# Attention with a Sinkhorn block sort, then a mixture of experts: one modality load, q ahead of v, and row scatters spread over attention units

## Chip, cores, metric

The kernel runs on one core of a Trainium2 chip. The metric is the device time of one execution in microseconds (us). Several executions are timed, and medians are given. An execution more than 1.5% above the fastest of the same kernel is called slow; the others are fast, and only fast ones enter a ratio. The ratio of two kernels is the mean time of one kernel's fast runs over the mean of the other's in the same rounds on the same chip, so it is not quite the ratio of the medians that are quoted beside it.

This case needs one more caution, which the experiments found: the chips, or something else that changes from one call of the experiments to the next, differ. In some calls the kernel before takes 244 to 247 us (medians), in others, on three other chips, 231 to 233. Every run below is therefore set against runs of the kernel before on its own chip, and the kind of chip is named.

## What is computed

The reference, cut to what matters:

```python
for _ in range(5):                                   # Sinkhorn, 32 (batch, head) pairs, 8x8 blocks
    P = softmax(P, axis=-1);  P = P / (P.sum(axis=-2) + 1e-9)
k_sorted = einsum('bhij,bhjcd->bhicd', P, k_blocks)  # same for v
attn = softmax(q_block @ k_sorted_block.T / 8)       # 96x96 blocks, head_dim 64
x = (attn @ v_sorted_block)  ->  3072 rows of 512
logits = x @ w_gate + modality_bias[modality_id]     # 8 experts
e_idx = argmax(logits);  gate = softmax(logits)[e_idx]
out[row] = gate * (relu(x[row] @ w1[e]) @ w2[e])     # 512 -> 1024 -> 512
```

## The kernel before

The work comes in two groups of 16 attention units (a unit is one head, half of its blocks, two batches). Group 0's k and v are sorted on PE, then units 0 to 15 run, with group 1's sort in between. Eight units make a chunk of 768 finished rows. For each chunk the kernel *chooses* the expert of each row on DVE, *ranks* the rows with matmuls (tile `rk`), writes them with eight indirect DMAs to an expert-ordered scratch in HBM, and computes from the expert counts a *table* of slots: blocks of 256 rows of one expert. A slot's rows come back by two transposing DMAs into `xT`. Hidden matmuls (`hp`) and output matmuls (`yp`) of the slots, "pieces", are put between the attention units from unit 17 on. Slots 0 and 1 come from chunk 0, 2 and 3 from chunk 1, 4 to 7 from chunk 2, 8 to 12 from chunk 3.

Loads at the start, all small ones on SP's queue, the large ones on POOL's:

```python
nc.sync.dma_start(out=P_t, ...)            # sort net
nc.sync.dma_start(out=BT[:, 0:2], ...)     # gate bias per modality, to all partitions, 8 KB
nc.sync.dma_start(out=wg_sb, ...)          # gate weights
for t in range(6):                         # modality ids, 4 bytes apiece
    nc.sync.dma_start(out=modI[...], in_=<every 12th id>)
...
load_k(0, 0); load_k(0, 1); load_v(0); load_q(0, 0); load_q(0, 1)
```

The first operations on `BT` are wedged between the Sinkhorn's own operations on DVE:

```python
gap = [ ..., [..., lambda: V.tensor_reduce(mA[:, 0:1], BT[:, 0], AX.X, ALU.max)], ...]
for it in range(5):
    nc.scalar.activation(P_t, P_t, ACT.Exp)
    for f in gap[it]:
        f()
    nc.vector.tensor_reduce(red, P_t, AX.X, ALU.add)   # ... the Sinkhorn goes on
```

The scatters of a chunk, one after the other on POOL, and the schedule:

```python
for t in range(8):
    if t:
        nc.gpsimd.nop()
    ins = nc.gpsimd.indirect_dma_start(out=xs_dram, out_offset=<dest[:, t]>, in_=<rows t>)
# ... cut
at2(8 * m + 9, place, m) if m == 0 else at1(8 * m + 10, place, m)
at1(8 * m + 10, table_x, m) if m == 0 else at2(8 * m + 10, table_x, m)
# after the loop:  at1(10, late_loads)

def late_loads():                          # second half of group 1's q, second expert's weights
    first = load_q(1, 1)
    tc.add_manual_dep(first.ins, xins[0].ins.name, SYNC, reason="rows of the first slot go ahead")
    load_w(1)
```

`at1(u, ...)` is the place in unit u ahead of its attention-value product, `at2` the one behind.

The softmax here doesn't subtract the row's maximum and nothing guards it: scores larger than these inputs give would overflow.

## Time and profile before

| | before |
|---|---|
| median of 3 runs | 245.98 us (245.48 to 247.62) |
| profiled span, mean granted clock | 243.9 us, 0.82 |
| PE busy | 70% |
| DMA packets under 512 B | 21,951 of 33,247 |

Two rows of the page, the engines' busy time and the chain of work that ended last, complete what the prediction shows:

```profile
PE 170.2 (70%) x2011; PEld 124.3 (51%) x2022; DVE 103.6 (42%) x344; ACT 91.9 (38%) x145; POOL 72.5 (30%) x100
...
PE 49%; issue 9%; another core or an unknown queue 8%; DVE 4%; ACT 3%; DMA 1%; POOL 0%; POOLq 0%; DVEq 0%; ACTq 0%
```

PE is busy 70% of the span, yet the chain has only half of its time on PE. "An unknown queue" at 8% means that an engine was released by an event which no recorded work explains: these are the late completion counts of PE that the prediction describes. (An engine raises a count, a semaphore, when an instruction is done, and the engines that need the result wait for this count. A count is called late where the trace records it well after the end of its instruction.)

### The profile page before, as it was taken

How to read it: one execution, taken by the hardware profiler on the slowest of the kernel's cores; microseconds unless marked ns; L12 is line 12 of the kernel's file. 1: busy time of each engine (PE TensorE's matmuls, PEld its weight loads, DVE VectorE, ACT ScalarE, POOL GpSimd, SP SyncE). 2: the span in 40 equal slices, each digit the busy share in tenths (PEclk: the TensorE clock that was granted, in tenths of full speed). 3: DMA queues.
4: the chain of work that ended last, by engine and by line, in shares of the span. 5: the costliest groups of instructions: out<-in, count | busy, mean ns of one | idle time of the engine just before them, and what ended most of it. 6: DMA issues, size and time to landing. Idle time of an engine off the chain costs nothing.

```text
span 243.9 us, 5078 instructions
## 1 busy us (share of the span) xinstructions
PE 170.2 (70%) x2011; PEld 124.3 (51%) x2022; DVE 103.6 (42%) x344; ACT 91.9 (38%) x145; POOL 72.5 (30%) x100
## 2 busy tenths in 40 slices
PE   0059619478544997929999854999990899999700
PEld 0059517377433886715766631667750467665300
DVE  6858626157720778502664703344630122232300
ACT  2028516536423685524624522354410323222200
POOL 7301070300074400473030571303275133223310
PEclk9999655558755579785999997699998699999975
DMA  5999999994022699524320223632053663222200
GB/s 81 214 222 176 213 226 196 217 209 77 0 69 66 102 187 208 103 81 108 84 89 3 102 81 78 157 60 89 17 171 119 135 155 84 86 86 78 82 26 0
DMA packets 33247, 27.64 MB, mean 113 GB/s; under 512 B 21951, under 2 KB 28863, under 8 KB 32960
## 3 DMA queue, kind: packets, MB, share of 16 engines
q0 software_dynamic: 11760, 23.10, 42.6%
q1 hardware_dynamic: 21456, 4.14, 10.8%
q8 instruction: 18, 0.29, 0.5%
q14 instruction: 13, 0.11, 0.1%
HBM read 27.33 MB, written 10.52 MB: 155 GB/s over the span
## 4 chain that ended last, share of the span: by engine, by line
PE 49%; issue 9%; another core or an unknown queue 8%; DVE 4%; ACT 3%; DMA 1%; POOL 0%; POOLq 0%; DVEq 0%; ACTq 0%
PE hp L624 18%; PE yp L647 17%; PE va L321 2%; PE gt L402 2%; PE lg L408 2%; PE op L389 2%; PE sc L370 2%; PE tq L354 1%; DMA xs_scratch<-xb,dest 1%; DVE xb L393 1%; ACT qT L618 1%; PE ypl L677 1%; PE hl L663 1%; ACT xTg L299 1%
## 5 line engine op out<-in xcount | busy, mean ns | idle before, releaser
L624 PE MATMUL hp<-xT,w 128*128 128x256 bf16 x384 | 50.2, 281 | 7.6 <-ACT qT L618 7.6
L638 POOL DMA_INDIRECT out_dram<-kvb,idg x25 | 24.4, 976 | 72.1 <-ACT kvb L634 30.4
L624 PEld LDWEIGHTS <-w 128*128 128x128 bf16 x384 | 37.0, 101 | 15.5 <-issue 7.8
L476 POOL DMA_INDIRECT xs_scratch<-xb,dest x32 | 29.3, 917 | 48.1 <-issue 48.1
L376 ACT ACTIVATE attnT<-sc 96x768 bf16<-96x768 f32 x32 | 25.7, 804 | 9.1 <-PE sc L370 3.5
L647 PE MATMUL yp<-w,qT 128*128 128x512 bf16 x91 | 25.1, 407 | 4.8 <-ACT qT L618 2.6
L647 PE MATMUL yp<-w,hT 128*128 128x512 bf16 x90 | 24.7, 414 | 0.3
L393 DVE TENSOR_TENSOR xb<-op,rs 96x512 bf16<-96x512 f32 x32 | 22.0, 687 | 1.1
L392 DVE RECIPROCAL rs<-op 96x8 f32<-96x8 f32 x32 | 6.4, 199 | 37.2 <-PE op L389 10.8
L618 ACT ACTIVATE qT<-hp 128x512 bf16<-128x512 f32 x16 | 9.4, 597 | 25.2 <-remote 13.3
L408 PE MATMUL lg<-wgp,xTg 128*96 128x8 bf16 x128 | 9.5, 198 | 13.2 <-ACT xTg L299 10.8
L634 ACT ACTIVATE kvb<-yp,idg 128x512 f32<-128x512 f32 x13 | 8.9, 686 | 24.0 <-PE yp L647 18.4
L636 DVE TENSOR_SCALAR kvb<-yp,idg 128x512 f32<-128x512 f32 x11 | 8.3, 751 | 22.8 <-PE yp L647 22.8
L299 ACT COPY qT<-tq 128x768 bf16<-128x768 bf16 x14 | 11.2, 797 | 17.0 <-PE tq L354 16.6
L647 PEld LDWEIGHTS <-qT 128*128 128x128 bf16 x96 | 9.3, 102 | 15.0 <-issue 4.4
L618 ACT ACTIVATE hT<-hp 128x512 bf16<-128x512 f32 x18 | 10.6, 594 | 15.5 <-PE hp L624 15.3
L389 PE MATMUL op<-v_sb,attnT 96*128 96x65 bf16 x256 | 16.0, 214 | 0.4 <-DVE xb L393 0.4
L408 PEld LDWEIGHTS <-xTg 128*96 128x96 bf16 x128 | 8.6, 146 | 14.5 <-ACT xTg L299 11.4
L354 PE MATMUL tq<-ident,q_il 128*128 128x128 bf16 x96 | 11.0, 271 | 6.9 <-DVE q_il L128 6.8
L389 PEld LDWEIGHTS <-attnT 96*128 96x128 bf16 x256 | 13.7, 111 | 3.4 <-DVE xb L393 0.7
L647 PEld LDWEIGHTS <-hT 128*128 128x128 bf16 x96 | 9.7, 105 | 10.4 <-issue 2.9
L370 PE MATMUL sc<-qT,kT 64*128 64x96 bf16 (+1 forms) x256 | 13.6, 237 | 1.6 <-DVE qT L299 0.7
(172 smaller groups left out, 219.7 us busy)
## 6 DMA issues: line engine op xcount, KB each, us to landing
w<-in_moe_w_dram POOLq DMA_DIRECT2D x4, 1024.0 KB
kvb<-in_k_dram POOLq DMA_DIRECT2D x4, 768.0 KB
kvb<-in_v_dram POOLq DMA_DIRECT2D x2, 1536.0 KB
v_sb<-in_q_dram POOLq DMA_DIRECT2D x4, 384.0 KB
q_in<-in_q_dram POOLq DMA_DIRECT2D x4, 384.0 KB
xs_scratch<-zpad SPq DMA_DIRECT2D x3, 258.0 KB
xs_scratch<-xb,dest POOLq DMA_INDIRECT x32
out_dram<-kvb,idg POOLq DMA_INDIRECT x25
```

Of the source, the lines that this page charges most:

```text
L299: (nc.scalar.copy if pick(act, dve) else nc.vector.tensor_copy)(dst, src)
L354: nc.tensor.transpose(tp[:, t], src[:, t], ident)
L370: nc.tensor.matmul(sc[0:m, par, j * BLK:(j + 1) * BLK], kT[g][rows, x0:x0 + m], qT[rows, i], start=True, stop=True)
L376: nc.scalar.activation(attnT[u % 2][:, 0:8 * BLK].rearrange("p (r f) -> p r f", r=2), sc_tiles.pop(u)[0:BLK, :, 0:4 * BLK], ACT.Exp, scale ...
L389: nc.tensor.matmul(ov[:, par, j], attnT[u % 2][:, c0:c0 + 128], v_sb[g][0:BLK, par * 64 + h * 8 + i, 0:D + 1], start=True, stop=True)
L393: nc.vector.tensor_tensor(xt[:, :, h * D:(h + 1) * D].rearrange("p (r j) d -> p r j d", r=2), ov[0:BLK, :, :, 0:D], rs.broadcast_to([BLK, ...
L408: nc.tensor.matmul(lg[:, t], xTg[c % 2][:, t], wgp[:, c], start=True, stop=True)
L476: ins = nc.gpsimd.indirect_dma_start(out=xs_dram, out_offset=bass.IndirectOffsetOnAxis(ap=dest[:, t:t + 1], axis=0), in_=xt.bitcast(I32)[: ...
L618: nc.scalar.activation(dst, src, ACT.Relu)
L624: nc.tensor.matmul(hp[:, f], w_at(s, c * F + (2 * j + f) * 128, 128), xT_b[s % NX][:, c], start=(c == 0), stop=(c == 3))
L638: ins = nc.gpsimd.indirect_dma_start(out=out, out_offset=bass.IndirectOffsetOnAxis(ap=idg[:, t, 0:1], axis=0), in_=y, in_offset=None, boun ...
L647: nc.tensor.matmul(yp, hT_b[s % 2][:, fc, t * 128:(t + 1) * 128], w_at(s, 4 * F + fc * Dm, Dm), start=(fc == 0), stop=(fc == 7))
```

## The change

The intent: the 4-byte modality pieces, which slow all other loads of the head, become one contiguous load and a transposition on PE; q comes ahead of v, so that attention starts before the v sort; and the eight scatters of a chunk, which stall PE's consumers when issued in a burst, leave one by one. The core of the diff:

```diff
     nc.sync.dma_start(out=P_t, ...)
+    modI = xTg[1].rearrange("p a b -> p (a b)").bitcast(I32)[0:NTL, 0:2 * BLK]
+    nc.sync.dma_start(out=modI, in_=<32 rows of 768 bytes>)
     nc.sync.dma_start(out=BT[:, 0:2], ...)
     nc.sync.dma_start(out=wg_sb, ...)
-    for t in range(6): nc.sync.dma_start(out=modI[...], ...)
...
+    load_q(0, 0)
     load_v(0)
-    load_q(0, 0)
     load_q(0, 1)
...
+            after = [mark[0].ins] if t else []          # mark: the last exponential or ReLU
+            for pre in after:
+                tc.add_manual_dep(ins.ins, pre.name, SYNC, reason="rows leave at an even pace")
...
-            at2(8 * m + 9, place, m) if m == 0 else at1(8 * m + 10, place, m)
-            at1(8 * m + 10, table_x, m) if m == 0 else at2(8 * m + 10, table_x, m)
-    at1(10, late_loads)
+            if m == 0:
+                at2(9, place, 0)
+                for t in range(1, 8):
+                    at1(9 + t, lambda t: ones_[0](t), t)
+                at1(16, table_x, 0)
+                at1(16, late_loads)
+            else:
+                at1(8 * m + 10, place, m)
+                for t in range(1, 8):
+                    (at2 if t % 2 else at1)(8 * m + 10 + t // 2, lambda t, m: ones_[m](t), t, m)
+                at1(8 * m + 14, table_x, m)
...
-    run_pieces(2)
+    for t in range(1, 8):
+        run_pieces(1)
+        ones_[3](t)
     table_x(3)
```

Cut: the transposition of the modality ids, the gate weights' product moved behind the k sort with its reduction on DVE, units 0 and 1 moved into the v sort, and a guard that holds a piece back while its slot has no table.

More of the change, by code (lines that the diff above doesn't have):

```diff
@@ L98 @@
     nc.sync.dma_start(out=P_t, in_=sort_net.rearrange("b h i j -> (b h) i j"))
+    mod_w = moe_modality_id.tensor.reshape(list(moe_modality_id.tensor.shape)).bitcast(I32).ap()
+    modI = xTg[1].rearrange("p a b -> p (a b)").bitcast(I32)[0:NTL, 0:2 * BLK]
+    nc.sync.dma_start(out=modI, in_=bass.AP(tensor=mod_w.tensor, offset=mod_w.offset,
+                                            ap=[[2 * BLK, NTL], [1, 2 * BLK]]))
     nc.sync.dma_start(out=BT[:, 0:2], in_=moe_modality_bias.rearrange("(o m) e -> o m e", o=1).broadcast_to([128, 2, E]))
@@ L101 @@
     nc.sync.dma_start(out=wg_sb, in_=moe_w_gate.rearrange("(c p) e -> p c e", p=128))
-    mod_w = moe_modality_id.tensor.reshape(list(moe_modality_id.tensor.shape)).bitcast(I32).ap()
-    modI = singles.tile([BLK, NTL], I32)
-    for t in range(6):
-        src = bass.AP(tensor=mod_w.tensor, offset=mod_w.offset + 2 * t,
-                      ap=[[12, 16], [2 * BLK, NTL], [1, 1]])
-        nc.sync.dma_start(out=modI[t * 16:(t + 1) * 16].rearrange("p (a o) -> p a o", o=1), in_=src)
     k_src = k.rearrange("b h (n c) d -> (b h n) (c d)", n=NB)
@@ L195, in perm_mult @@
         eng.tensor_tensor(tmp, a, p_, ALU.mult)
-        nc.vector.tensor_reduce(dst, tmp, AX.X, ALU.add)
+        return lambda: nc.vector.tensor_reduce(dst, tmp, AX.X, ALU.add)
     V = nc.vector
@@ L261, in home_map, with mod_rows @@
         nc.vector.tensor_tensor(perm, hb, sF8.broadcast_to([128, E, E]), ALU.is_equal)
-        perm_mult(BTp, BT, "b")
+        perm_mult(BTp, BT, "b")()
         nc.vector.tensor_copy(etab, BTp[0:1, 3])
     biasm = singles.tile([BLK, NTL, E], FP32)
+    modB = singles.tile([NTL, 6, 16], BF16)
     modF = singles.tile([BLK, NTL], FP32)
     modN = singles.tile([BLK, NTL], FP32)
+    def mod_rows():
+        src = modI.rearrange("b (r t w) -> b t r w", r=16, t=6)[:, :, :, 0]
+        nc.vector.tensor_copy(modB, src)
+        tp = mipsum.tile([128, 64], BF16, tag="mi", name="modT")
+        nc.tensor.transpose(tp[0:BLK, 0:NTL], modB.rearrange("b t r -> b (t r)"), ident[0:NTL, 0:NTL])
+        nc.vector.tensor_copy(modF, tp[0:BLK, 0:NTL])
+    wgf = small.tile([128, 4, E], FP32, tag="wgf", name="wgf")
     def gate_consts():
-        wgf = small.tile([128, 4, E], FP32, tag="wgf", name="wgf")
-        perm_mult(wgf, wg_sb, "w")
-        nc.gpsimd.tensor_copy(wgp, wgf)
-        nc.gpsimd.tensor_copy(modF, modI)
+        red_w = perm_mult(wgf, wg_sb, "w")
         nc.gpsimd.tensor_scalar(modN, modF, -1.0, 1.0, ALU.mult, ALU.add)
@@ L282, in gate_consts, with rest_w @@
         nc.gpsimd.tensor_tensor(biasm, biasm, tmp, ALU.add)
+        def rest_w():
+            red_w()
+            nc.vector.tensor_copy(wgp, wgf)
+        return rest_w
     busy = [0.0, 0.0]
@@ L375, in expo @@
     def expo(u):
-        nc.scalar.activation(attnT[u % 2][:, 0:8 * BLK].rearrange("p (r f) -> p r f", r=2),
+        mark[0] = nc.scalar.activation(attnT[u % 2][:, 0:8 * BLK].rearrange("p (r f) -> p r f", r=2),
                              sc_tiles.pop(u)[0:BLK, :, 0:4 * BLK], ACT.Exp, scale=scale)
@@ L439 @@
     scat = {}
+    ones_ = {}
+    mark = [None]
     def place(m):
@@ L472, in place, with one @@
         use(dve=1.5)
-        for t in range(8):
+        def one(t):
             if t:
@@ L478, in place @@
                 in_=xt.bitcast(I32)[:, t], in_offset=None)
-            tc.declare_no_dep(ins.ins, group="xs", reason="rows are disjoint")
+            after = [mark[0].ins] if t else []
+            tc.declare_no_dep(ins.ins, group="xs", reason="rows are disjoint", **({"keep": after} if after else {}))
             tc.add_to_no_dep_group("xs", ins.ins)
+            for pre in after:
+                tc.add_manual_dep(ins.ins, pre.name, SYNC, reason="rows leave at an even pace")
             scat[m].append(ins.ins)
+        ones_[m] = one
+        one(0)
         nxt = ohs[(m + 1) % 2]
@@ L615, in relu @@
         if not pick(0.61, 0.7):
-            nc.vector.tensor_scalar(dst, src, 0.0, None, ALU.max)
+            mark[0] = nc.vector.tensor_scalar(dst, src, 0.0, None, ALU.max)
         else:
-            nc.scalar.activation(dst, src, ACT.Relu)
+            mark[0] = nc.scalar.activation(dst, src, ACT.Relu)
     def mL1(s, j):
@@ L701 @@
     use(dve=0.5)
+    mod_rows()
     make_upper_triangular(nc, maskUT, val=1.0, diag=False)
@@ L704 @@
     g0 = jobs(0, [s_, o_, m_, m_, m_, m_, s_, o_,
-                  m_, m_, s_, m_, m_, o_, m_, m_, m_, m_, o_, m_, m_])
+                  m_, m_, o_, m_, m_, o_, m_, m_, o_, m_, m_, o_])
+    hold = []
     for n, (f, g, x0, kd) in enumerate(g0):
@@ L710 @@
             use(dve=2.0)
+            load_k(1, 0)
+            load_k(1, 1)
+            hold.append(gate_consts())
+            prep_s(0)
+            prep_q(0)
+            prep_q(1)
+            scores(0)
+            expo(0)
             make_bd(1)
             late_consts()
-            load_k(1, 0)
-            load_k(1, 1)
-        if n == 13:
-            prep_s(0)
-        if n == 16:
-            prep_q(0)
-            scores(0)
-            expo(0)
+        if n == 12:
+            scores(1)
+            expo(1)
+    hold[0]()
     load_v(1)
@@ L723 @@
     load_w(0)
-    gate_consts()
-    prep_q(1)
     zero_block()
@@ L797, in run_pieces @@
             f, a = pieces[st["pos"]]
+            if (f is mL1 and a[0] >= st["x"]) or (f is last_L1 and SL >= st["x"]):
+                return
             f(*a)
@@ L811 @@
         p1, p2 = pace(u)
-        if u:
+        if u > 1:
             scores(u)
```

## The prediction

> **What bounds the kernel now.** I read the page first, then the chain of waits, then stretches of the timeline. The page says that TensorE (PE) is the busiest engine, but in bands:
>
> ```profile
> PE   0059619478544997929999854999990899999700
> PEclk9999655558755579785999997699998699999975
> DMA  5999999994022699524320223632053663222200
> ```
>
> PE's row has holes (slices 6, 8, 12, 24, 31), and the clock row drops to half around each. I asked for engine busy time in six stretches that the timeline shows without matmuls:
>
> ```profile
> core 0: us, PE busy (x) PEld busy (x) DVE busy (x) ACT busy (x) POOL busy (x), PEclk, DMA share, GB/s
> 30.80:36.00 5.20, 0.03 (x1) 0.00 (x0) 1.01 (x4) 0.80 (x1) 4.34 (x7) 0.50 1.12 225
> 45.30:50.10 4.80, 0.00 (x0) 0.00 (x0) 1.02 (x3) 1.10 (x2) 2.46 (x6) 0.50 1.19 224
> 70.30:76.70 6.40, 0.05 (x1) 0.05 (x2) 0.00 (x0) 1.89 (x3) 4.84 (x6) 0.50 0.29 82
> 105.40:109.80 4.40, 0.00 (x0) 0.00 (x0) 0.00 (x0) 1.60 (x2) 3.49 (x4) 0.85 0.31 90
> 143.20:150.30 7.10, 2.17 (x14) 0.79 (x14) 1.11 (x3) 1.24 (x3) 3.39 (x4) 0.94 0.25 70
> 182.50:190.20 7.70, 0.06 (x2) 0.03 (x1) 0.47 (x1) 0.68 (x2) 3.54 (x4) 0.79 0.44 133
> ```
>
> Length less PE busy: 5.2 + 4.8 + 6.3 + 4.4 + 4.9 + 7.6 = 33.2 us of idle PE. The waits name them:
>
> ```profile
> DVE wgf L196 <- POOL ptmpw L195: 4.2, 1, 4.2
> POOL modF L273 <- DMA modI<-in_moe_modality_id_dram: 10.5, 1, 10.5
> ACT qT L618 <- remote: 13.3, 2, 8.1
> DVE qT L616 <- remote: 10.3, 1, 10.3
> ```
>
> Hole one: the gate weights' product stands in POOL's queue behind loads that wait for the v sort. Hole two: the modality ids (2 KB pieces, 20.5 us to landing) end at 46.4. The other four are the four bursts of eight row scatters, one burst per chunk of attention. In burst one:
>
> ```profile
> 70.91 0.91 POOL L476 DMA_INDIRECT xs_scratch<-xb,dest  x1 [0.30 <-issue]
> 75.75 0.91 POOL L476 DMA_INDIRECT xs_scratch<-xb,dest  x1 [0.30 <-issue]
> 76.65 0.80 PE L408 MATMUL lg<-wgp,xTg 128*96 128x8 bf16 x8 [6.35 <-ACT xTg L299]
> 78.59 1.34 SPq L591 DMA_TRANSPOSE xT<-xs_scratch  x1
> 78.67 0.20 DVE L392 RECIPROCAL rs<-op 96x8 f32<-96x8 f32 x1 [9.69 <-PE va L321]
> ```
>
> DVE waits 9.7 us for a matmul group that ended at 70.30. In the trace's semaphore records, PE's completion counts normally appear at once; during a burst they appear at 69.98, 72.89, 75.78 and 78.64, one per 2.9 us, while ACT's and DVE's own counts are prompt. So consumers of PE starve, then PE. Output scatters 1.9 us apart (123.91, 125.82) delay nothing.
>
> **What the Trainium skill says.** "DMA: Bandwidth & Descriptors", Rules for kernel authors: a non-contiguous last dimension becomes one descriptor per element. The trace agrees: about 3,200 packets of 4 bytes, nearly all between 18 and 48 us. Same page, Queues, rings and completion order: an engine alternates between queues at packet granularity. The trace agrees: these small packets drain only as fast as the large loads beside them. "SBUF — State Buffer", SBUF: two separate sides: only DVE and GpSimd share a port, as a lock. That does not explain the bursts: ACT also stalls, and DVE ran its table arithmetic during 177.0 to 179.3, beside scatters. "TensorE: Matmul & The Clock Gate", Part 1: the clock halves after an idle window of about 3.4 us and recovers after a busy one. The drops agree; recovery here takes 3.6 us (190.2) to 11.3 us (76.7).
>
> **The change, part by part**, on that trace's clock.
>
> *Head.* Modality becomes one load of 32 rows, transposed on PE (about 0.4 us before the k sort); hole two, 4.8 us, goes. The gate product moves early; hole one goes as a wait. But q's first half now precedes v in one queue. Before, v landed at 19.97, q's first half at 24.83; the same bytes in the new order put v at about 25. The v sort started at 20.4; I now start it at 25.6, after the first scores (home map 2.0 us, spread 0.6, transposes, copies). Its remaining 55 matmuls at half clock take 0.12 us each (20 took 2.37), so it ends, with the second scores, at 33.6 instead of 30.2. Then evacuation, reduce, spread: unit 2's scores at 37.6 instead of 38.43. Gain **0.8**, not 5. With the modality, **5.6**.
>
> *Chunk 0.* One scatter per unit: burst one's 6.3 goes, and sooner recovery of the clock gives perhaps 1.5. Units 11 to 16 then end **13.5** earlier.
>
> *The price of spreading.* The last of those scatters waits for unit 16's exponential, which ends at T (92.6 before, 79 after). Before, the last scatter (75.75) to the first slot's transposed rows (81.76) took 6.0 us. The first slot's matmuls come 0.85 us after T in PE's order, so PE waits about 5.2 us. The second half of group 1's q waits for those rows too: it is issued 0.6 us later, and landed 8.4 us after issue (82.36 to 90.78), so at T+15.1. DVE's spread of it stands ahead of chunk 1's choice: 0.6 + 1.5 us more, the rank matmuls at T+17.3. They were at T+5.4 (97.98): **−11.9**. From there to the second slot's first matmul took 16.4 us with burst two in it; without it, at half clock at first, about 12.8: **+3.6**. Net so far **+5.2**.
>
> *Chunk 1.* Scatters every half unit to unit 21, table in unit 22, rows needed in unit 23. Table arithmetic 1.75 us, address load 1.3, transposed rows 3.2: about 2 us late. **−2**.
>
> *Chunk 2.* Its table moves from unit 26 to unit 30, but its slot 4 was due in unit 29, so the new guard skips unit 29's pieces. The last scatter waits on unit 29's exponential and queues behind two output scatters; PE then waits 7 us for slot 4. Burst three's 4.9 us hole and its half clock go, a 7 us hole and its half clock come: **about 0**.
>
> *Chunk 3.* Scatters alternate with pieces of 0.9 or 1.7 us, and two output scatters lie between: ten on POOL at 1.2 us, nearly a burst again, though each waits for a relu and so throttles itself. Rank matmuls to slot 8 took 22.0 us; I get 15 to the last scatter plus 6.1, so 21, followed by half clock as before: **0 to −1**.
>
> Strict sum: 5.2 − 2 − 0.5, about 2.7, so 243. I chose 241: several debits are taken in full, while a PE without holes in the first 60 us could regain full clock earlier (it ran at 0.5 from 26.5 to 57.2), each window of 3.4 us of it worth 1.7.
>
> **Rivals.** (1) The holes simply go: 33 us less, and some clock: 210 to 215. For it: the scatters' pace is slower than any that stalled. Against: the program order above. It needs row loads and q to be early, and they are moved late. (2) Late rows and late q cost more than the bursts did: 250 or more. For it: 11.9 + 2 + 7 + 6 nearly equals the 23 us of bursts. Against: the modality wait and burst one go for certain, and little takes their place. (3) Even spread scatters delay PE's counts: a few us worse everywhere; the output scatters speak against it. (4) Loads bound the head: then removing 3,000 small packets matters. The page has DMA at 9 tenths to slice 8, but the k sort and v sort of group 1 run well after their data land (36.2, 43.6), so only v of group 0 is affected.
>
> **Range and chances.** The clock (±3), the slot 0 chain (±3), chunks 2 and 3 (±4 together) give about ±6, somewhat wider downward, as rival 1 is partly right if q lands sooner. 2% faster is 241.06, just beside my number: faster 0.47, same 0.46, slower 0.07.
>
> **What would show it.** Right: no wait on the modality load; the v sort starting near 25; no "remote" waits of 5 us or more in the attention; PE waiting 4 to 6 us at the first hidden matmuls, then DVE waiting 6 to 8 us for q's load at unit 17; a hole of about 6 us before slot 4 and one before slot 8. Wrong: rows of slot 0 in time, q landing within 4 us of issue, a v sort not later than before, or full clock through the early units, each worth 3 to 8 us below my number; or PE's counts still late with spaced scatters, above it.

## The result

Median 255.91 us (254.38 to 256.43, 4 runs) against 246.59 us (245.48 to 247.62, 4 runs) for before on the same chip; ratio 1.0368, 95% interval 1.0297 to 1.0439. The change makes the kernel 3.7% slower. The profiled spans are 254.7 and 243.9 us.

The page of the changed kernel, same rows as before:

```profile
PE 170.7 (67%) x2012; PEld 123.6 (49%) x2023; DVE 102.7 (40%) x344; ACT 93.0 (37%) x147; POOL 72.7 (29%) x98
...
PE   0007687957799182998599961399975499999600
PEclk9999589975559656799869997599999579999975
DMA  6999968999111299931511222442134843222200
...
PE 54%; DMA 14%; DVE 13%; ACT 5%; issue 4%; another core or an unknown queue 3%; SPq 1%; POOL 1%; POOLq 0%; DVEq 0%; ACTq 0%
```

PE does the same work. The early holes (before: slices 6, 8 and 12) are gone, but there are new ones at slices 14, 16, 25 to 26 and 31 to 32. In the chain "unknown queue" fell from 8 to 3%, but DMA rose from 1 to 14% and DVE from 4 to 13%. The summary of waits names them (columns: total us, times, longest):

```profile
PE hp L641 <- DMA xT<-xs_scratch: 20.1, 4, 9.9
PE rep L238 <- DVE P_bf L232: 18.3, 1, 18.3
...
PE rk L459 <- DVE oh L443: 7.6, 3, 5.6
...
DVE q_il L125 <- DMA q_in<-in_q_dram: 5.7, 1, 5.7
ACT attnT L385 <- remote: 5.7, 1, 5.7
...
DVE mA L204 <- DMA BT<-n_moe_modality_bias_dram: 4.0, 1, 4.0
```

The first line says that the hidden matmuls wait four times for rows, 20.1 us in all; in before this view has no such line. The last is a wait in the Sinkhorn. The timeline (start, duration, engine, line, work, and in brackets the idle time ahead of it and what ended it) shows the two most costly places:

```profile
89.18 1.87 PE L641 MATMUL hp<-xT,w 128*128 128x256 bf16 x8 [3.97 <-DMA xT<-xs_scratch]
...
89.73 1.62 POOL L118 DMA_DIRECT2D q_in<-in_q_dram  x2 [5.85 <-DMA xT<-xs_scratch]
...
98.29 0.63 DVE L125 COPY q_il<-q_in 128x768 bf16<-128x768 bf16 x2 [5.68 <-DMA q_in<-in_q_dram]
...
100.37 0.23 PE L459 MATMUL rk<-oh,maskUT 96*128 96x64 bf16 x1 [5.60 <-DVE oh L443]
...
157.85 0.81 ACT L385 ACTIVATE attnT<-sc 96x768 bf16<-96x768 f32 x1 [5.67 <-remote]
...
163.35 1.87 PE L641 MATMUL hp<-xT,w 128*128 128x256 bf16 x8 [9.89 <-DMA xT<-xs_scratch]
```

The first slot's rows reach PE 4.0 us late; behind them q's second half is issued at 89.73 and usable at 98.29, and the rank matmuls of chunk 1, in DVE's order behind the copy of q, start at 100.37. The last line is slot 4, rows 9.9 us late. Ahead of it in the program the scatters of chunk 2 and of the output stand in one row on POOL (150.3, 151.6, 152.8, 154.1, 155.4), and PE's counts are late again: in the semaphore records the counts of a score matmul that ended at 153.36 and of the table's matmul at 153.47 were seen 4.4 and 4.3 us after them. So the wait "remote" of 5.67 is the old illness, in a scatter sequence that was meant to cure it.

Where the span went, in sections, from the traces (T is the end of unit 16's exponential; "slot s" the first ReLU of slot s). Positive is a loss. The last column is the same pair of kernels on a chip without late counts:

| section | predicted | measured | on a chip without late counts |
|---|---|---|---|
| start to T | −13.5 | 92.6 → 82.7: −9.9 | 84.8 → 80.9: −3.9 |
| T to slot 1 | +8.3 | 23.3 → 28.9: +5.6 | 19.0 → 28.5: +9.5 |
| slot 1 to slot 2 | +2 | 10.6 → 16.7: +6.1 | 10.6 → 11.9: +1.4 |
| slot 2 to slot 4 | 0 | 30.8 → 37.0: +6.2 | 28.8 → 31.3: +2.6 |
| slot 4 to slot 8 | 0 to +1 | 38.4 → 38.2: −0.1 | 36.1 → 36.4: +0.3 |
| slot 8 to the end | 0 | 48.3 → 51.2: +2.9 | 51.2 → 49.2: −2.0 |

The last section has the same work in both kernels. Asked for engine busy time from slot 8's first matmul to the end, the traces answer, before and after (columns as in the prediction):

```profile
194.50:243.90 49.40, 35.29 (x229) 22.26 (x231) 11.07 (x16) 10.28 (x17) 11.66 (x12) 0.91 0.24 74
```

```profile
201.50:254.70 53.20, 37.87 (x228) 23.41 (x232) 10.24 (x15) 10.37 (x17) 10.68 (x11) 0.85 0.25 70
```

The same matmuls keep PE busy 2.6 us longer at a granted clock of 0.85 instead of 0.91. On the other chip this section went the other way, so it is put down to the phase in which the clock drops fell, not to a part of the change. No run tests that.

### The profile page after: what moved, and what is told of

It reads as the page before. It is cut to its first block, busy times and chain, and to the rows that moved or that the text cites. A ratio compares the mean times of both kernels' runs of the same rounds, so it can differ in the third digit from the quotient of the medians.

```text
span 254.7 us, 5091 instructions
## 1 busy us (share of the span) xinstructions
PE 170.7 (67%) x2012; PEld 123.6 (49%) x2023; DVE 102.7 (40%) x344; ACT 93.0 (37%) x147; POOL 72.7 (29%) x98
## 4 chain that ended last, share of the span: by engine, by line
PE 54%; DMA 14%; DVE 13%; ACT 5%; issue 4%; another core or an unknown queue 3%; SPq 1%; POOL 1%; POOLq 0%; DVEq 0%; ACTq 0%
PE hp L641 17%; PE yp L664 14%; DMA xT<-xs_scratch 5%; PE va L330 4%; DMA BT<-n_moe_modality_bias_dram 3%; PE gt L411 3%; DMA q_in<-in_q_dram 3%; PE lg L417 3%; PE ka L321 3%; PE op L398 3%; PE sc L379 2%; DMA xs_scratch<-xb,dest 2%; DVE xb L402 2%; PE tq L363 2%
## 5 line engine op out<-in xcount | busy, mean ns | idle before, releaser
L641 PE MATMUL hp<-xT,w 128*128 128x256 bf16 x384 | 56.0, 301 | 23.0 <-DMA xT<-xs_scratch 20.1
L641 PEld LDWEIGHTS <-w 128*128 128x128 bf16 x384 | 39.6, 107 | 34.5 <-issue 17.6
L635 ACT ACTIVATE hT<-hp 128x512 bf16<-128x512 f32 x19 | 11.3, 597 | 40.1 <-PE hp L641 39.7
L664 PE MATMUL yp<-w,qT 128*128 128x512 bf16 x91 | 23.6, 391 | 1.6 <-ACT qT L635 1.2
L664 PE MATMUL yp<-w,hT 128*128 128x512 bf16 x90 | 22.7, 386 | 2.5 <-ACT qT L635 2.1
L635 ACT ACTIVATE qT<-hp 128x512 bf16<-128x512 f32 x17 | 10.0, 597 | 20.5 <-PE hp L641 10.6
L651 ACT ACTIVATE kvb<-yp,idg 128x512 f32<-128x512 f32 x14 | 9.6, 685 | 18.7 <-PE yp L664 16.5
L653 DVE TENSOR_SCALAR kvb<-yp,idg 128x512 f32<-128x512 f32 x10 | 7.5, 750 | 21.1 <-PE yp L664 21.1
L330 PE MATMUL va<-bd,kvb 128*128 128x128 bf16 x128 | 14.5, 284 | 1.0 <-DVE v_sb L308 0.6
L398 PEld LDWEIGHTS <-attnT 96*128 96x128 bf16 x256 | 13.5, 110 | 3.4 <-DVE xb L402 0.8
L308 ACT CAST v_sb<-va 96x512 bf16<-96x512 f32 (+1 forms) x19 | 11.8, 657 | 7.8 <-PE va L330 6.9
L330 PEld LDWEIGHTS <-kvb 128*128 128x128 bf16 x128 | 13.1, 189 | 1.4 <-issue 1.1
L379 PE MATMUL sc<-qT,kT 64*128 64x96 bf16 (+1 forms) x256 | 12.8, 227 | 0.7 <-ACT qT L308 0.2
```

Of the source, the lines that this page charges most:

```text
L308: (nc.scalar.copy if pick(act, dve) else nc.vector.tensor_copy)(dst, src)
L330: nc.tensor.matmul(acc[:, z], v_cols[:, d0 + z], bd[g], start=True, stop=True)
L379: nc.tensor.matmul(sc[0:m, par, j * BLK:(j + 1) * BLK], kT[g][rows, x0:x0 + m], qT[rows, i], start=True, stop=True)
L398: nc.tensor.matmul(ov[:, par, j], attnT[u % 2][:, c0:c0 + 128], v_sb[g][0:BLK, par * 64 + h * 8 + i, 0:D + 1], start=True, stop=True)
L635: mark[0] = nc.scalar.activation(dst, src, ACT.Relu)
L641: nc.tensor.matmul(hp[:, f], w_at(s, c * F + (2 * j + f) * 128, 128), xT_b[s % NX][:, c], start=(c == 0), stop=(c == 3))
```

## The experiments

Theory A: three delays that the change itself makes (the gate-bias table behind the modality load; q's second half behind the first slot's rows; late tables in the later chunks) outweigh what the head and the bursts give. Rival B: spread scatters as such hold the engines. Rival C: the new order of the large loads is the cost. All results are correct. Chips: the first call ran on a chip with late counts, all later calls on three chips without; the changed kernel was first measured on a chip with late counts, perhaps the same one.

| run | edit, in words | median, us | before on that chip | ratio (95%) |
|---|---|---|---|---|
| e1_bt_first | changed kernel, gate-bias table first | 248.35 | 244.01 | 1.0147 (1.0058–1.0236) |
| e2_head_only | head of the change alone | 241.75 | 244.01 | 0.9934 (0.9864–1.0004) |
| e3_spread_only | spreading alone | 255.61 | 244.01 | 1.0439 (1.0352–1.0527) |
| e4_q_early | changed kernel, q's second half early | 244.11 | 244.01 | 0.9976 (0.9888–1.0064) |
| e5_bt_q | both repairs | 228.47 | 231.37 | 0.9932 (0.9825–1.0039) |
| e6_spread_c0 | both, only chunk 0 spread | 227.14 | 231.37 | 0.9859 (0.9765–0.9954) |
| e7_bursts | both, all in bursts | 225.42 | 231.37 | 0.9779 (0.9665–0.9893) |
| e8_two | as e7, at most two in flight | 240.81 | 231.37 | 1.043 (1.027–1.059) |
| e9_after | changed kernel | 240.06 | 232.22 | 1.033 (1.0246–1.0414) |
| e10_bt_q | as e5 | 229.06 | 232.22 | 0.9858 (0.9777–0.9939) |
| e11_bursts | as e7 | 225.0 | 232.22 | 0.9714 (0.9629–0.9799) |
| e12_before | before, for its trace | 232.16 (one run) | 232.22 | – |
| e13_c23_burst | changed kernel, chunks 2 and 3 in bursts | 238.57 | 231.66 | 1.0185 (1.0087–1.0283) |
| e14_modality | before, contiguous modality load fourth | 234.11 | 231.66 | 1.0076 (1.0004–1.0147) |
| e15_bursts | as e7 | 224.91 | 231.66 | 0.9697 (0.9614–0.978) |
| e16_flights | as e7, another number in flight per chunk | 244.05 (one run) | 231.66 | – |
| e17_modality_third | before, contiguous modality load third | 226.97 | 232.47 | 0.9765 (0.968–0.9849) |
| e18_defer | as e7, no pieces in units 29 and 30 | 219.35 | 232.47 | 0.9368 (0.9266–0.947) |

The profiled executions of e1, e4, e13 and e18 were slow.

**e1_bt_first**

```diff
-    nc.sync.dma_start(out=modI, ...)
     nc.sync.dma_start(out=BT[:, 0:2], ...)
+    nc.sync.dma_start(out=modI, ...)
```

> The changed kernel with the gate-bias table's load put back ahead of the modality load. Theory A (the loss is a sum of three delays that the change itself makes: the gate-bias table late in the Sinkhorn, the rows of the first slot and the second half of q late after unit 16, and the tables of the later chunks late): the table lands near 4.5 us, the block matrix is ready near 15.3 instead of 19.3, and the total falls by 3 to 4 us, to about 252. It falls less if the modality load, now later, is waited for instead (it is read just before the k sort). Rival B (spread scatters as such hold the engines) and rival C (q ahead of v is the cost): no change, 255 to 256.

From 1.0368 to 1.0147 of before: 2.2%, or 5.4 us of 244. The wait on the table is gone, and the Sinkhorn's last product releases PE 4.1 us earlier than the 18.3 shown above:

```profile
PE rep L238 <- DVE P_bf L232: 14.2, 1, 14.2
```

T comes at 79.0 instead of 82.7, and the modality load, now third, lands 4.1 us after issue and is waited for by nobody. The fast profile of the same head (e10) has the same 14.2. The two ratios come from two calls, perhaps two chips; e9 and e10 below repeat the shift on one. Theory A holds here; B and C, which expected nothing, fall for this part.

**e2_head_only and e3_spread_only**

```diff
 e2: the scatter loop, the places of place, table_x and late_loads as in the kernel before
 e3: the kernel before with the new scatter loop, its places, late_loads at unit 16, the guard
```

> The changed kernel's head, with the scatters, tables and late loads as they were before. Theory A: the gain of 5.7 us at unit 6 stays, with the four bursts as before, so about 241 (240 to 242). Rival C (the new order of the loads in the head is the cost): 250 or more. Rival B: also about 241, as the spread scatters are gone.

> The kernel before with the spread scatters and their tables alone, head untouched. Theory A and rival B: the spreading costs what the change lost less what its head gained, about 15 us: 258 to 262. Rival C: 246 or faster, as the head is the old one.

The head alone is 0.7% faster (the interval just includes no gain), the spreading alone, with q's second half held back as in the change, 4.4% slower, and 0.9934 × 1.0439 = 1.037, the change itself. So the loss is in the second half of the change; rival C falls as the main cause. The head brought the start of unit 6's exponential from 54.6 to 48.9, against the trace of before from the first measurement. How much of that is left at the end is open: within the call the means differ by about 1.6 us (0.7% of 244), while the one execution profiled, the fastest of four, has a span 5.5 us below that older trace. The four bursts are there in both kernels. The summary of waits of e2 has, for one of them, 10.1 us with no recorded releaser:

```profile
DVE qT L628 <- remote: 10.1, 1, 10.1
```

**e4_q_early**

```diff
     load_q(1, 0)
     load_w(0)
+    load_q(1, 1)
+    load_w(1)
...
-                at1(16, late_loads)
```

> The changed kernel with the second half of group 1's q and the second expert's weights loaded right behind the first expert's, not behind the rows of the first slot. Theory A: DVE's wait of 5.7 us for q at unit 17 goes; the rank matmuls of chunk 1 come near T+10 instead of T+17.7 (T is the end of unit 16's exponential), what is left being the wait for the first slot's rows; total 248 to 251, less if the added 2.7 MB hold up the loads of group 1's k and v. Rival B: nothing to gain from q, 254 to 256.

From 1.0368 to 0.9976: 3.9%, or 9.6 us, the largest single piece. (The edit loads the second expert's weights early too; the wait that goes is the one for q.) The wait for q is gone, and in its profile the rank matmuls come at T+11.6. PE's counts were still over 4 us late in chunk 2. The fast pair e9 and e10 below shows the same.

**e5_bt_q, e6_spread_c0, e7_bursts, e8_two**

```diff
 e5: e1 and e4 together
 e6: + for t in range(8 if m in (1, 2, 3) else 1): one(t)      # and the tables of before
 e7: + the same with chunk 0
 e8: e7, and  + after = [scat[m][t - 2]] if t >= 2 else []     # waits for a landing
```

> The changed kernel with both repairs: the gate-bias table first, and q's second half with the second expert's weights loaded early. Theory A: the two delays lie one after the other, so their gains add (7.6 and 11.8 us in the medians): 236 to 240. If they overlap (both only move the same wait), 243 to 245.

> Both repairs, and only chunk 0 spread; chunks 1 to 3 scatter in bursts with their tables as before. Theory A: chunks 1 to 3 lost about 13 us between unit 22 and slot 8 to late tables, and the bursts there cost less than that: 5 to 10 us below the run with both repairs, 229 to 234. Rival B' (the spreading of chunks 1 to 3 is worth its late tables): at or above the run with both repairs.

> Both repairs, all four chunks in bursts as before. Theory A: 237 (the head-only run's 241.75 less the 4 us of the gate-bias table), and some 6 us above the run with only chunk 0 spread, as burst one returns.

> As the run of four bursts, but each scatter of a burst waits until the one two before it has landed, so at most two row scatters are in flight. Theory: three or more in flight delay PE's completion counts; with two the counts come within 1 us and the holes of 4 to 6 us at the four bursts shrink to under 2, total 222 to 228. Rival (POOL's descriptor work itself delays the counts, whatever is in flight): counts late as in the bursts, total as the bursts or 1 to 3 us worse, as the rows leave later.

The absolute numbers expected were for a chip like the first. This one takes 231.37 for the kernel before, and no PE count in any of the four traces is over 0.1 us late. So the run of two in flight can't tell what it was made for. It tells another thing: holding scatters back until others land costs 15 us, because rows come late (31.1 us of such waits, 15.6 in e7):

```profile
PE hp L643 <- DMA xT<-xs_scratch: 31.1, 4, 10.8
```

Bursts stand at 0.9779, spreading chunk 0 alone at 0.9859 and spreading all at 0.9932, 1.5% above the bursts. The 5 to 10 us that spreading chunks 1 to 3 was expected to lose did not appear: 1.3 us in the medians, within the intervals. And the bursts are 1.7 us below the run with chunk 0 spread, where 6 above it were expected.

**e9_after to e12_before**: the changed kernel, e5, e7 and before on one chip, unedited.

> The changed kernel itself again, as the last call ran on a chip where the kernel before takes 231 us, not 246, and where no PE count came late. On a chip with late counts: 1.037 of before again. On a chip without: the bursts cost before nothing, so spreading has nothing to win and its late tables and late q stand alone: 1.05 or more of before (243 to 248 against 231).

> Both repairs again (gate-bias table first, q early), beside the changed kernel on the same chip. Gains of 4 to 7 (table) and 6 to 12 us (q) measured apart; if they add: 15 to 19 us below the changed kernel of this call; if they overlap: 10 to 12.

> Both repairs with all scatters in bursts. On a chip with late counts the bursts cost 4 to 8 us each, so this is within 4 us of the run with both repairs and spread scatters, on either side; on a chip without late counts, about 3 us below it, as in the last call.

> The kernel before, for its trace on this chip. If this chip times it near 246, DVE's wait for the attention product in burst one is 8 to 10 us and the semaphore records show PE's counts 4 us or more late in each of the four bursts; if it times it near 231, no such wait is over 3 us, and the stretch without matmuls in burst one is under 3 us instead of 6.3.

Again a chip without late counts. The stretch that the prediction shows as burst one with 0.05 us of PE work reads in e12, same program and same scatters:

```profile
70.30:76.70 6.40, 6.03 (x72) 5.24 (x72) 3.56 (x9) 3.81 (x7) 4.60 (x6) 0.51 0.27 79
```

```profile
73.67 0.20 DVE L392 RECIPROCAL rs<-op 96x8 f32<-96x8 f32 x1 [2.09 <-PE op L389]
```

PE works through the burst, and DVE's longest wait in it is 2.1 us, not 9.7. Of 14 traces of the later calls, none has a PE count over 0.1 us late. Until the first scatter the two traces of before agree within 0.2 us (unit 10's exponential at 66.2 and 66.0); they part only from burst one on. So the burst's cost goes with the chip, or with the call, and not with the program, and the change still costs 3.3% where there is no such cost to remove (5% or more was expected).

The changed kernel on this chip (e9), then with both repairs (e10):

```profile
98.73 0.24 PE L459 MATMUL rk<-oh,maskUT 96*128 96x64 bf16 x1 [6.37 <-DVE oh L443]
...
150.72 1.86 PE L641 MATMUL hp<-xT,w 128*128 128x256 bf16 x8 [7.78 <-DMA xT<-xs_scratch]
```

```profile
82.56 1.87 PE L641 MATMUL hp<-xT,w 128*128 128x256 bf16 x8 [3.83 <-DMA xT<-xs_scratch]
...
138.63 1.86 PE L641 MATMUL hp<-xT,w 128*128 128x256 bf16 x8 [7.82 <-DMA xT<-xs_scratch]
```

With the repairs T moves from 80.9 to 76.5 (−4.4, the table) and chunk 1's rank matmuls from 98.7 to 88.0 (−10.7: 4.4 and then 6.3 for q). That is the whole of the 11.0 us between the medians, so in this trace the two shifts lie one behind the other. But 11.0 is below the 15 to 19 that was expected if the gains add, and in the 10 to 12 that was expected if they overlap. On this chip neither repair was run alone, so that the gains add is not shown. The slot-4 wait is the same, 7.8 us: nothing there was repaired. The bursts (e11) are 4.1 us better still.

**e13_c23_burst** (changed kernel; bursts and old tables for chunks 2 and 3)

> The changed kernel with chunks 2 and 3 in bursts and their tables as before; nothing repaired. If the spreading of these two chunks is what the prediction mis-sized: the hole before slot 4 falls from 9.9 us (7.8 on a chip without late counts) to 6 or less, and the total is 5 to 8 us below the changed kernel where counts come late (248 to 251 against 255.9), 3 to 5 us below it where they don't (235 to 237 against 240). If the loss lies in chunks 0 and 1 and is only carried on: within 1 us of the changed kernel.

1.0185 against 1.033 for the changed kernel on the same chip: 1.4%, 3.4 us, just clear of the two intervals taken together; 3 to 5 were expected. In its profile slot 4 waits 6.45 us, as in the fast profile of e15 below, not 7.78. So the spreading of these chunks, with the later tables that go with it, costs time even where counts are prompt. Half of this run's executions were slow, so the size is less sure than its sign.

**e14_modality and e17_modality_third**

```diff
-    for t in range(6): nc.sync.dma_start(out=modI[...], ...)
+    nc.sync.dma_start(out=modI, in_=<32 rows of 768 bytes>)   # e14 behind wg_sb, e17 ahead of it
+    mod_rows()                                               # the transposition, ahead of the k sort
```

> The kernel before with the one contiguous modality load alone, behind the gate-bias table. The prediction's step says hole two, 4.8 us, goes: 4 to 6 us below the kernel before, with the matmuls of chunk 0's first gate group no longer waiting 4.9 us. If the loads bound the head anyway (rival 4): within 1 us of before.

> The kernel before with the one contiguous modality load alone, third on its queue: behind the gate-bias table, ahead of the gate weights. Step of the prediction: 4.8 us at hole two, so 4 to 6 us below before, with no wait of PE near 50 us. Rival (another wait takes its place, such as the gate weights, which now land later): within 1.5 us of before.

In e14 I put the load fourth, behind the gate weights, not where its expectation says. It is no faster than before. The list of DMA issues (KB each, median us from issue to landing) and the timeline say why:

```profile
xTg<-in_moe_modality_id_dram SPq DMA_DIRECT2D x1, 24.0 KB, 18.3
```

```profile
20.60 0.23 DVE L269 CAST modB<-xTg 32x96 bf16<-32x96 int32 x1 [5.33 <-DMA xTg<-in_moe_modality_id_dram]
```

The load landed at 20.6, after v at 20.2, and the transposition, ahead of the k sort on PE, waited for the cast: the k sort started at 21.1 instead of 15.3. What held it was the gate weights ahead of it: in the DMA records they are 512 packets of 32 bytes, from 4.3 to 19.9 us, and the last list says why they take so long. One place earlier (e17):

```profile
xTg<-in_moe_modality_id_dram SPq DMA_DIRECT2D x1, 24.0 KB, 4.2
```

and this part alone makes the kernel 2.35% faster, 5.5 us, with unit 6's exponential 4.5 us earlier than in e12. Unit 2's is 0.5 us later, so the gain is at hole two and not in the loads ahead of it: rival 4 of the prediction falls. The gate weights, now fourth, land 18.7 us after issue, and the summary of waits has no line for them.

**e15_bursts and e16_flights**

> Both repairs with all scatters in bursts, a third time, for a chip with late counts if this is one: there about 237, 0.96 to 0.975 of before; on a chip without, 225 again, 0.97 to 0.98.

> Both repairs, bursts, but in chunk 0 a scatter waits until the one before has landed, in chunk 1 the one two before, in chunk 2 the one three before; chunk 3 free. If the chip has late counts and the number in flight is the cause: no count over 1 us late in chunks 0 and 1, 2 to 4 us in chunk 2, 5 or more in chunk 3. If the descriptor work of POOL is the cause: late in all that issue within 1.3 us, so in chunks 1 to 3 alike. On a chip without late counts it tells nothing of this; there the waits alone cost, 8 to 20 us above the bursts.

The bursts repeat (0.9697). For e16 the chip again had prompt counts; with one scatter at a time in chunk 0, PE waited 20 us for slot 0's rows. It says nothing on the cause of late counts.

**e18_defer**

```diff
-        return (1, 1) if u >= 17 else (0, 0)
+        return (1, 1) if u >= 17 and u not in (29, 30) else (0, 0)
```

> Both repairs, all scatters in bursts, and no hidden pieces in units 29 and 30, so the first pieces of slot 4 come behind attention that doesn't need its rows; the same pieces then stand before slot 8. If the program order makes the waits: the holes of 6.4 us before slot 4 and 5.3 before slot 8 fall under 2 each, total 5 to 9 us below the run of bursts: 216 to 220 where before takes 232, about 0.94; where counts come late, 228 to 234 against 246. Rival (the chain through chunk 3 sets the end, whatever fills PE): the wait moves behind it, within 2 us of the bursts, 0.97.

The waits for rows ahead of slots 4 and 8 in e15, and then in e18:

```profile
134.04 1.87 PE L643 MATMUL hp<-xT,w 128*128 128x256 bf16 x8 [6.42 <-DMA xT<-xs_scratch]
...
170.41 3.60 PE L643 MATMUL hp<-xT,w 128*128 128x256 bf16 x16 [5.42 <-DMA xT<-xs_scratch]
```

```profile
136.92 1.86 PE L643 MATMUL hp<-xT,w 128*128 128x256 bf16 x8 [3.11 <-DMA xT<-xs_scratch]
...
167.44 2.77 PE L643 MATMUL hp<-xT,w 128*128 128x256 bf16 x16 [1.97 <-DMA xT<-xs_scratch]
```

They halve at least, though they don't fall under 2 us each, and the two fast runs stand at 0.937 of before (the other two of the four were slow). PE did wait because slot 4's matmuls stood ahead of attention that had its data. This version beats both kernels. It was run only on a chip with prompt counts; on one with late counts it is untested.

## Why the prediction was wrong

It said 241, give or take about 6 and somewhat more downward; the result was 255.9, beyond that and on the side given 7%. Its main mechanism, late rows and late q eating what the holes give back, was right, and rival 2 came true by its figure. Rival 2's own sum, 11.9 + 2 + 7 + 6 = 26.9, lies 4 us above the 23 of bursts that it was said nearly to equal. (A slip without effect: the list of slices leaves out slice 18, burst two, which the table of stretches has.) The steps that failed are a term missing in the head, the worth of burst one, and chunks 1 and 2, where spread scatters were taken to delay no count. By its own steps:

- **"Head. ... Gain 0.8, not 5. With the modality, 5.6."** A term is missing here. The new modality load went ahead of the gate-bias table. The table landed 8.5 us after issue, and DVE, in order, stood 4.0 us in the Sinkhorn. The v sort started at 30.0, not 25.6. I had looked at what the new load brings and not at what it pushes back. Without that term (e1) unit 2's exponential gains 1.9 us, and unit 6's 9.3, against 0.8 and 5.6. In the changed kernel itself unit 2's came 1.8 later, yet unit 6's 5.7 earlier: that this meets the 5.6 is luck, a gain sized too small and a delay left out. The modality part alone is 4.5 (predicted 4.8), against e12.
- **"Units 11 to 16 then end 13.5 earlier."** They ended 9.9 earlier; with the table repaired 13.6 (T at 79.0 in e1, as predicted). Two errors cancel there: the head was 3.7 us too small, and from unit 6 to T the gain was 4.3, not the 7.8 of a hole of 6.3 and some clock. It was 4.2 in the changed kernel, so its whole shortfall at T lies in this stretch. Against e2, which has the new head and the bursts, the stretch is 6.0 us shorter, near the hole; with the new head and bursts it takes 1.8 us longer than in before, which the step left out. Why is open.
- **"The price of spreading": about right.** PE waited 4.0 us at the first slot (said: about 5.2), q was copied behind a wait of 5.7 (said: 6 to 8), the rank matmuls came at T+17.7 (said: T+17.3). To slot 1 the section lost 5.6, where 8.3 was said.
- **"Chunk 1. −2."** It lost 6.1. Where counts are prompt it lost 1.4. In the first pair of traces PE's counts were up to 3.65 us late around 112 to 116, with row and output scatters 1.3 us apart. That they made the difference is argued, not tested.
- **"Chunk 2 ... Burst three's 4.9 us hole and its half clock go, a 7 us hole and its half clock come: about 0." This step failed most in size.** It lost 6.2. Without late counts the wait for slot 4 is 7.8 us, near the 7 worked out, and the section loses 2.6. With them it is 9.9. The step took it that a spread sequence delays no count, though it itself said that the last scatter "queues behind two output scatters". Five of them in a row at 1.25 us made a burst again. "Rival (3)" was put aside with a pair of scatters 1.9 us apart, which says nothing of that spacing. So rival 3 came true in part, and with it the prediction's own sign of an error above its number, "PE's counts still late with spaced scatters". e13 shows that undoing chunks 2 and 3 gains 3.4 us even without late counts.
- **"Chunk 3 0 to −1": right by its total** (a gain of 0.1), although PE's counts were up to 7.5 us late there as well.
- **The choice of 241 instead of the strict 243** rested on the clock. It was 0.833 on average against 0.82, but the time after slot 8 ran at 0.85 instead of 0.91 and lost 2.9. The hope had no row of the profile behind it.

In sum, against the strict gain of 2.7: 3.6 less at T, 2.7 more to slot 1, 4.1, 6.2 and 2.9 less at the later sections, and 0.6 more in chunk 3 make the loss of 10.8 in the spans.

What the change would have given, on the chips with prompt counts: both repairs with bursts stand at 0.970 to 0.978; spreading takes 1.4 to 1.5% from that, the late q and the late table the rest down to 1.033. With late counts, once fully repaired, spreading is not measured. The nearest pair, both with the table late: spread with q early (e4) stands at 0.9976, bursts (e2) at 0.9934, within the intervals. So even there the spreading, with its late tables, won nothing that these runs can see.

Still open: why PE's counts come late, and whether the number in flight or the pace matters. No later call drew a chip of that kind, and chip and call can't be told apart for it.

## What to carry to other kernels

When a small load is put ahead of another one, look up who waits for the one that moves back; here a wait of 4.0 us inside DVE moved T by 3.7 to 4.4 us. Spreading work over time also moves all that depends on its last piece: follow the last scatter, not the average, to the rows, the table and the loads tied to them. And before tuning against a stall, see whether it appears on another chip.

## What the Trainium skill lacked or had wrong

- "DMA: Bandwidth & Descriptors", SWDGE vs HWDGE vs iDMA, tells that indirect DMAs are issued from GpSimd. Neither this page nor another has that PE's completion counts can be seen late beside them: up to 7 to 10 us in each of the four bursts in the traces of before (first measurement) and e2, none over 0.1 us on the three chips of the later calls, with the program of before among them. The kernel before takes 244.0 to 246.6 us there and 231.4 to 232.5 here. No page says that chips differ so.
- "SBUF — State Buffer", The DMA setup-cost knee, gives every transfer roughly 2 us fixed. The trace agrees for loads issued before the bulk (the sort net 1.5 to 1.8 us, the modality load 1.7 to 1.8 when second). What it lacks is what small loads cost beside bulk loads: the modality load took 4.1 to 4.6 us as third, behind the gate-bias table, and 18.3 as fourth, behind the gate weights, though the issues are under half a microsecond apart; the gate-bias table 2.7 to 3.4 as second and 8.5 to 8.6 as third.
- "DMA: Bandwidth & Descriptors", Queues, rings and completion order, has alternation between queues at packet granularity. The trace agrees closely: in before POOL's and SP's queues moved 226 packets each from 6 to 12 us and 98 each from 12 to 18. What the page lacks is an example of what follows. A small load's time went by the number of its own packets and of those ahead of it on its queue, and by the size of the other queue's packets: the gate weights, 512 packets of 32 bytes, landed 18.4 to 18.7 us after issue with v (packets of 12 KB) ahead of q, and, fourth, after 11.6 to 13.7 with q (768 bytes) ahead of v.
- No page has a figure for an indirect row scatter: one of 96 rows took 2.4 to 3.1 us (medians of the runs) from issue to landing, and letting each wait for the one two before it cost 15 us in the whole kernel.
